# Natural-order loads of k and v, 64-row transposes and a direct wq product in a retention and token-mixing kernel

## The chip, the cores and the metric

The kernel runs on one core of one Trainium2 chip. The metric is device time in microseconds (us), the median of several runs of one launch. Profiled times come from one execution taken by the hardware profiler; its span begins and ends a little inside the time that is measured for the run.

## The reference

A recurrent retention layer (4 batches, 8 heads, 768 tokens, head size 64) is followed by a token-mixing layer on the 512 joined features. Inputs and output are 32-bit floats.

```
for t in range(S):                      # S = 768, per batch and head
    state = gamma[h] * state + outer(k[t], v[t])
    y[t]  = scale * q[t] @ state
x     = y, heads joined                 # (4, 768, 512)
wq, wk = x @ w_q, x @ w_k               # 512 -> 64
W_tok = scale * wq @ wk.T               # per batch, 768 x 768
out   = relu(W_tok @ x) @ w_out         # 512 -> 512
```

## The kernel before

The recurrence is computed in chunks of 128 tokens. Two chunks make a pair (256 tokens); there are 3 pairs in a batch and 12 in all, numbered 0 to 11. The decay factors are folded into v before the products and into y after them, so that within a chunk a masked matrix of scores does the work and between chunks a running state of 64x64 per head. The mixing layer never forms W_tok: z = wk.T @ x is summed over a batch's three pairs, and each pair's output follows from wq and z.

Every unit of work is a short named step of one pair. The list ORDER, written out in the file, is the order of the steps in the program: `name.pair.part:engine@bank`, with engines A (ScalarE, ACT in the profile), V (VectorE, DVE) and P (GpSimd, POOL); steps without a letter are matmuls (TensorE, PE). Each engine runs its own instructions strictly in this order, and waits where data or a buffer are not there. The steps of one pair, in the order in which data flow:

- `ck`, `cv`, `cq` cast k, v and q to 16 bits; `cv` also multiplies by the decay table `fv` (line 316, the other casts go through the helper of lines 137 and 138).
- `trk`, `trq` (lines 344, 359) transpose k and q on TensorE, 8 transposes of 128x128 each into one PSUM bank, and `ekT`, `eqT` copy them to SBUF.
- `sc` (line 379) makes the scores, `eat` (line 391) masks them with `cmask`; `st` (line 433) adds to the state, `es` copies it; `ia` (453) and `in` (419) make y from the scores and from the state; `ex` (467) scales y into `x`.
- `xt` (483) and `exT` transpose x. `wqk` (497) makes wq and wk in 8 matmuls; `ewq` and `ew` copy them out, `ewq` twice side by side; `tw` (523) transposes wq in two transposes and `ewt` copies the result.
- `zm` (545) and `ez` make z once per batch; `mx` (565), `r` (580, 582), `pj` (587) and `eo` make the output rows of a pair. `fill` (292) is matmuls on zeros, which keep TensorE active. `W` and `WO` cast weights.

Loads and stores go out on SyncE's queue (SP), in the order of the list LOADS: `k4` is a load of 512 KB, `w` and `o` are the weights, `s3` is a store of one pair's output. A load is written into one of 18 staging buffers, and is placed in the program behind the cast that frees the buffer. Each load reads runs of 512 bytes: two neighbouring tokens of one head lie side by side in one partition,

```
            in_=src[b, xs.start * HP : xs.stop * HP, cp * 2 * C : (cp + 1) * 2 * C, :].rearrange(
                "h (g j) d -> g h (j d)", j=2
```

so partition g holds tokens 2g and 2g+1 of the pair, and a chunk of 128 tokens lies in 64 partitions. The casts of k and v therefore take a chunk in two pieces of 64 partitions (even and odd tokens), and place these into the lower and the upper 64 partitions of the result. For every pair that is 4 instructions for k and 4 for v. Scores and masks use the same order of tokens (even ones first).

Of the kernel before, what the change touches and what calls it, by code (L numbers as in the profile page):

```python
# [16 lines left out]
ck.0.1:V cq.0.0:A ck.0.0:P fill.20@6 trk.0@6 cq.0.1:V trq.0@0 cv.0.0:V ekT.0:A eqT.0:A st.0.0  # L17
ck.1.1:V ck.1.0:A cv.0.1:P sc.0.0@0 eat.0.0:V es.0.0:A sc.0.1@2 eat.0.1:V fill.1@6 trk.1@6
cq.1:A fill.3@0 trq.1@0 st.0.1 cv.1.0:P ia.0.1@2 ekT.1:A ck.2.0:A in.0.1@2 eqT.1:V ia.0.0@2
sc.1.0@0 es.0.1:A sc.1.1@4 cq.2:A ck.2.1:P st.1.0 ex.0:V trk.2@6 cv.1.1:P trq.2@2 eat.1.1:V  # L20
es.1.0:A eat.1.0:V eqT.2:A ekT.2:V ck.3.1:A ck.3.0:A xt.0@4 st.1.1 sc.2.0@2 cv.2.0:P cq.3:A
sc.2.1@0 exT.0:V es.1.1:V cv.2.1:P ia.1.0@4 cv.3.0:P in.1.0@4 eat.2.0:V in.1.1@4 ia.1.1@4
cv.3.1:P ck.4.1:P ex.1:V st.2.0 in.2.0@2 fill.1@6 trk.3@6 es.2.0:A cv.4.0:P cv.4.1:P fill.1@4
trq.3@4 ekT.3:A eat.2.1:V W:A ia.2.0@2 eqT.3:V ia.2.1@2 in.2.1@2 xt.1@6 sc.3.0@4 ex.2:V st.3.0
wqk.0@0 xt.2@1 exT.1:A wqk.1@6 es.3.0:A sc.3.1@2 eat.3.0:V ewq.0:A in.3.1@4 exT.2:V st.3.1
wqk.2@1 ew.0:A cq.4:A ia.3.0@4 eat.3.1:V ewq.1:A ewq.2:V ew.2:V ia.3.1@4 tw.1@2 ex.3:V cv.5.0:P
ew.1:A ck.4.0:A trq.4@6 trk.4@3 tw.0@1 ewt.1:V tw.2@0 es.3.1:A ck.5.1:A ekT.4:V eqT.4:V ck.5.0:A
ewt.2:A xt.3@4 st.4.0 cq.5:A fill.2@2 sc.4.0@2 trk.5@6 ewt.0:A exT.3:V ekT.5:V zm.0@4 trq.5@5
ez.0:A cv.5.1:P WO:P sc.4.1@0 es.4.0:A eat.4.0:V st.4.1 cq.6:P mx.0@2 eat.4.1:V eqT.5:A cv.6.0:P
es.4.1:A sc.5.1@4 sc.5.0@0 r.0:A wqk.3@6 st.5.0 eat.5.1:V in.4.0@2 mx.2@4 eat.5.0:V ewq.3:A  # L30
ia.4.1@2 in.4.1@2 es.5.0:V ck.6.1:A ck.6.0:A r.2:A cv.6.1:P ia.4.0@2 ew.3:V ia.5.1@0 in.5.0@0
ex.4:V in.5.1@0 ia.5.0@0 ex.5:V pj.0.0@6 trk.6@2 xt.4@3 trq.6@4 ekT.6:V pj.0.1@5 eo.0.0:A xt.5@6
eqT.6:V mx.1@0 exT.4:A exT.5:V ck.7.0:A sc.6.0@2 eat.6.0:V ck.7.1:P r.1:A st.6.0 cv.7.0:P tw.3@4
pj.2.0@6 cq.7:A wqk.4@0 es.6.0:V ew.4:V eo.2.0:A sc.6.1@2 wqk.5@1 trq.7@6 eat.6.1:V ewt.3:A
trk.7@4 ew.5:V ewq.4:A st.6.1 ewq.5:A ekT.7:V cv.7.1:P eqT.7:A pj.1.0@1 tw.4@6 es.6.1:V eo.0.1:V
ia.6.1@2 ck.8.1:A eo.1.0:A ia.6.0@2 in.6.1@2 cv.8.1:P sc.7.0@4 ewt.4:V cq.8:A st.7.0 zm.1@6
sc.7.1@0 ex.6:V trq.8@2 es.7.0:A eat.7.0:V cv.8.0:P ez.1:A xt.6@6 ck.8.0:A pj.1.1@3 exT.6:V
eat.7.1:V trk.8@4 pj.2.1@6 mx.4@0 eqT.8:A eo.1.1:A mx.3@2 st.7.1 r.4:V ekT.8:A sc.8.0@4 eo.2.1:A
ck.9.1:P wqk.6@6 es.7.1:A cq.9:P r.3:A st.8.0 ck.10.0:P ewq.6:A ia.7.1@0 ew.6:A ia.7.0@0
sc.8.1@2 in.7.0@0 es.8.0:A in.7.1@0 eat.8.0:V cq.10:P eat.8.1:V in.8.0@4 ck.9.0:A in.8.1@4  # L40
pj.4.0@6 eo.4.0:A ck.10.1:A ex.7:V cv.9.0:P ia.8.0@4 ia.8.1@4 pj.3.0@2 tw.5@6 cv.9.1:P trk.9@3
ex.8:V ewt.5:A trq.9@0 trq.10@6 eqT.9:V eqT.10:V ekT.9:A xt.8@4 sc.9.0@0 eat.9.0:V st.9.0
trk.10@3 eo.3.0:A ekT.10:V pj.4.1@6 exT.8:A ck.11.0:P sc.9.1@0 ck.11.1:A mx.5@4 es.9.0:V
eat.9.1:V xt.7@3 wqk.8@2 eo.4.1:A trk.11@6 ia.9.1@0 r.5:A exT.7:A cq.11:P ia.9.0@0 in.9.1@0
ewq.8:V cv.10.0:P ew.8:A sc.10.0@4 cv.10.1:P st.9.1 tw.6@3 ekT.11:V cv.11.0:P wqk.7@6 trq.11@2
ex.9:V ewt.6:A tw.8@3 eat.10.0:V ew.7:A es.9.1:A eqT.11:A ewq.7:A ewt.8:V pj.3.1@0 eo.3.1:V
xt.9@1 sc.11.0@2 sc.10.1@4 exT.9:A pj.5.1@6 pj.5.0@1 tw.7@0 st.10.0 eat.11.0:V eat.10.1:V
eo.5.0:V eo.5.1:A ewt.7:V zm.2@6 es.10.0:A ez.2:A st.10.1 es.10.1:V in.10.1@4 sc.11.1@2
cv.11.1:P in.10.0@4 mx.6@0 ia.10.1@4 eat.11.1:V r.6:A wqk.9@6 ia.10.0@4 st.11.0 mx.7@0 ex.10:V
r.7:A pj.6.0@2 eo.6.0:A es.11.0:V ewq.9:V ia.11.1@4 ew.9:A ia.11.0@4 in.11.0@4 in.11.1@4 mx.8@0  # L50
xt.10@6 pj.6.1@2 ex.11:V exT.10:A xt.11@3 r.8:A wqk.10@6 eo.6.1:V exT.11:V pj.7.1@4 ew.10:V
ewq.10:V eo.7.1:A wqk.11@3 ew.11:A tw.9@6 pj.7.0@2 ewq.11:A tw.10@3 ewt.10:V zm.3@4 ewt.9:A
pj.8.0@6 ez.3:V tw.11@3 eo.7.0:A eo.8.0:A mx.10@4 mx.9@0 ewt.11:V mx.11@2 pj.8.1@6 r.10:A
pj.10.1@4 r.11:V pj.10.0@5 eo.10.1:V pj.11.1@2 pj.11.0@4 eo.8.1:A eo.10.0:A r.9:V pj.9.0@6
eo.9.0:A pj.9.1@5 eo.11.0:V eo.9.1:A eo.11.1:V
# [5 lines left out]
q0 v0 k1 q1 v1 k2 q2 v2 k3 q3 v3 w k4 q4 v4 k5 q5 v5 o k6 q6 v6 k7 q7 v7 k8 q8 v8 k9 q9 v9 k10  # L61
q10 s0 v10 k11 s1 q11 s2 v11 s4 s3 s5 s6 s7 s8 s10 s11/0 s11/1 s9
# [3 lines left out]
OBUFS = 10  # L66


@with_exitstack
def kernel(  # L70
# [9 lines left out]
):  # L80

# [9 lines left out]
    C = 128  # L91
# [27 lines left out]
    wqn_pool = pool("wqn", 3)  # L119
# [8 lines left out]
    def bank16(b):  # L128
        return banks[:, b, :].bitcast(BF16)
# [19 lines left out]
    def load(name, p, half=None, eng=None):  # L149
        src = {"k": k, "q": q, "v": v}[name]  # L150
        b, cp = divmod(p, NP)
        st = pairs[p]
        if name + "_st" not in st:
            st[name + "_st"] = stage_pool.tile([128, 2, HP, 2, D], FP32, name=name + "_st", tag="st")
        xs = slice(0, 2) if half is None else slice(half, half + 1)
        dma = (eng or nc.sync).dma_start(
            out=st[name + "_st"][:, xs].rearrange("g x hp j d -> g (x hp) (j d)"),
            in_=src[b, xs.start * HP : xs.stop * HP, cp * 2 * C : (cp + 1) * 2 * C, :].rearrange(
                "h (g j) d -> g h (j d)", j=2
            ),  # L160
        )
    def load_token(token):
        if token == "w":
            nc.sync.dma_start(out=wq_stage, in_=moe_w_q.rearrange("(a p) h -> p a h", p=128))
            nc.sync.dma_start(out=wk_stage, in_=moe_w_k.rearrange("(a p) h -> p a h", p=128))
        elif token == "o":
            for a in range(NDM):
                nc.sync.dma_start(
                    out=wout_stage[:, a], in_=moe_w_out[128 * a : 128 * a + 128, :], max_dma_last_dim=512
                )  # L170
        else:
            load(token[0], int(token[1:]))
# [10 lines left out]
    def more_loads():  # L183
        while queue:
# [6 lines left out]
            if token not in "wo":  # L191
                n = len(staged)
                if n >= STAGES and staged[n - STAGES] not in cast:
                    return
                staged.append(token)
# [53 lines left out]

    identity = const_pool.tile([128, 128], BF16, name="identity")  # L250
# [24 lines left out]
    wqk_sb = const_pool.tile([128, NDM, 2 * DH], BF16, name="wqk_w")  # L275
    wout_sb = const_pool.tile([128, NDM, DM], BF16, name="wout_sb")

    def W(e):
        copy(e, wqk_sb[:, :, 0:DH], wq_stage)
        if e == "A":  # L280
            nc.scalar.mul(out=wqk_sb[:, :, DH:], in_=wk_stage, mul=float(wk_scale))
        else:
            ENGINES[e].tensor_scalar_mul(
                out=wqk_sb[:, :, DH:], in0=wk_stage, scalar1=float(wk_scale)
# [14 lines left out]
    def ck(e, b, p, c):  # L299
# [3 lines left out]
        for j in range(2):  # L303
            copy(
                e,
                st["ks"][rows(j), c].rearrange("p hp x d -> p x hp d"),
                st["k_st"][rows(c), :, :, j],
# [3 lines left out]
    def cv(e, b, p, c):  # L311
        st = pairs[p]
        if "vs" not in st:
            st["vs"] = cast_pool.tile([128, 2, HP, 2, D], BF16, name="vs")
        for j in range(2):
            ENGINES[e].tensor_tensor(  # L316
                out=st["vs"][rows(j), c].rearrange("p hp x d -> p x hp d"),
                in0=st["v_st"][rows(c), :, :, j],
                in1=fv[rows(c), p % NP, :, j]
                .rearrange("p (x hp) -> p x hp", x=2)  # L320
                .to_broadcast([G, 2, HP, D]),
                op=ALU.mult,
            )
        release("v" + str(p), 2)
# [13 lines left out]

    def trk(e, b, p):
        st = pairs[p]  # L340
        ps = bank16(b).rearrange("p (hp c t) -> p hp c t", hp=HP, c=2)
        for c in range(2):
            for hp in range(HP):
                nc.tensor.transpose(  # L344
                    ps[:, hp, c], st["ks"][:, c, hp].rearrange("p x d -> p (x d)"), identity
                )
        st["ktr_ps"] = bank16(b)

    def ekT(e, b, p):
        st = pairs[p]  # L350
        st["kT"] = qkt_pool.tile([128, HP, 2, C], BF16, name="kT")
        copy(e, st["kT"].rearrange("p hp c t -> p (hp c t)"), st["ktr_ps"])

    def trq(e, b, p):
        st = pairs[p]
        ps = bank16(b).rearrange("p (hp c j g) -> p hp c j g", hp=HP, c=2, j=2)
        for hp in range(HP):
            for j in range(2):
                nc.tensor.transpose(  # L359
                    ps[:, hp, :, j, :],  # L360
                    st["qs"][:, hp, j].rearrange("p x d -> p (x d)"),
                    identity,
                )
        st["qtr_ps"] = bank16(b)

    def eqT(e, b, p):
        st = pairs[p]
        st["qT"] = qkt_pool.tile([128, HP, 2, C], BF16, name="qT")
        copy(e, st["qT"].rearrange("p hp c t -> p (hp c t)"), st["qtr_ps"])
# [18 lines left out]
    def eat(e, b, p, half):  # L388
# [5 lines left out]
            in1=cmask.rearrange("p o j t -> p o (j t)").to_broadcast([128, 8, C]),  # L394
# [271 lines left out]
```

## Time and profile before

| | before |
|---|---|
| median of 3 runs | 102.04 us (101.32 to 102.66) |
| the profiled execution, its time | 101.49 us |
| its span | 99.8 us |
| mean granted TensorE clock | 0.955 |
| busy: PE, DVE, ACT, POOL | 86.5, 75.3, 72.5, 66.8 us |
| packets of the load and store queue | 52592, 26.22 MB |
| read from and written to HBM | 20.19 MB and 6.29 MB |

The busy times are those of instructions on an engine, the share is of the span. Matmuls overlap each other, so their mean durations are latencies; how fast they follow each other is read from the chain of waits, where each piece runs from its release to the next one's. DMA rates are given in GB/s over a stretch, and the DMA share is the time of packets over sixteen engines, which goes above 1 where a packet starts before the one ahead has ended.

### The profile page before, as it was taken

Reading aid. Unit: us, or ns where it says so; the run is one execution under the profiler, and the core shown is the slowest. Engines: PE = TensorE matmul, PEld = TensorE weight load, DVE = VectorE, ACT = ScalarE, POOL = GpSimd, SP = SyncE. Lnnn points to the kernel's source line nnn. Section 1 sums busy time; section 2 is a strip of 40 time slices with the busy share of each in tenths; the row PEclk is TensorE's granted clock in tenths of the full one; section 3 lists DMA queues with packets and bytes.
Section 4 is the critical chain, followed back from the end, with each engine's and each line's share of the span. In section 5 each row is a group of like instructions: output and inputs, shape, how many; then the busy total and the mean of one; then the engine's idle time right before and its main releaser. Section 6 shows DMA issues by size and latency. Waiting matters only on the chain.

```text
span 99.8 us, 3208 instructions
## 1 busy us (share of the span) xinstructions
PE 86.5 (87%) x1319; PEld 60.0 (60%) x1332; DVE 75.3 (75%) x114; ACT 72.5 (73%) x123; POOL 66.8 (67%) x82
## 2 busy tenths in 40 slices
PE   4994669968999899989987999999899999999920
PEld 1344537857798666666865667768666776644400
DVE  3066972999999899967989678999969988227800
ACT  4126977199799996799899998999784567754130
POOL 6566589998969689769999999995699930000000
PEclk9999955699999999999999999999999999999995
DMA  1999999999999999999999999899967600762995
GB/s 22 283 348 347 347 347 349 285 253 276 323 298 295 327 290 322 270 312 336 338 343 346 323 300 305 255 317 341 290 204 217 204 13 7 210 210 69 317 290 167
DMA packets 53134, 26.68 MB, mean 267 GB/s; under 512 B 1920, under 2 KB 53120, under 8 KB 53120
## 3 DMA queue, kind: packets, MB, share of 16 engines
q1 hardware_dynamic: 52592, 26.22, 89.5%
q10 hardware_dynamic: 528, 0.26, 0.9%
q8 instruction: 10, 0.16, 0.6%
q14 instruction: 4, 0.03, 0.1%
HBM read 20.19 MB, written 6.29 MB: 265 GB/s over the span
## 4 chain that ended last, share of the span: by engine, by line
PE 41%; DVE 23%; DMA 14%; ACT 10%; issue 5%; SPq 1%; POOL 1%; ACTq 0%; DVEq 0%; POOLq 0%
PE banks L587 16%; DVE at_sb L391 11%; DMA q_st<-in_q_dram 7%; DMA v_st<-in_v_dram 6%; PE banks L453 4%; ACT ks L137 4%; DVE x_nat L467 4%; PE banks L483 3%; PE banks L379 3%; ACT o_st L137 3%; PE banks L497 2%; DVE vs L316 2%; PE banks L359 2%; PE banks L419 2%; PE banks L433 2%
## 5 line engine op out<-in xcount | busy, mean ns | idle before, releaser
L316 POOL TENSOR_TENSOR vs<-v_st,fv 64x512 bf16<-64x512 f32 x46 | 48.9, 1062 | 8.3 <-DMA v_st<-in_v_dram 3.7
L391 DVE TENSOR_TENSOR at_sb<-banks,cmask 128x1024 bf16<-128x1024 f32 x24 | 28.8, 1218 | 0.6 <-ACT s_sb L137 0.4
L587 PE MATMUL banks<-wout_sb,relu 128*128 128x512 bf16 x86 | 22.5, 379 | 0.8 <-ACT wqn L137 0.2
L137 ACT CAST ks<-k_st 64x512 bf16<-64x512 f32 x30 | 18.6, 619 | 1.8 <-DMA k_st<-in_k_dram 1.5
L467 DVE TENSOR_TENSOR x_nat<-banks,fy 128x1024 bf16<-128x1024 f32 x12 | 14.5, 1220 | 2.1 <-PE banks L453 1.1
L137 ACT COPY o_st<-banks 128x512 f32<-128x512 f32 x17 | 10.0, 589 | 6.6 <-PE banks L587 6.4
L587 PEld LDWEIGHTS <-relu 128*128 128x128 bf16 x96 | 8.5, 98 | 8.5 <-issue 0.8
L137 ACT CAST qs<-q_st 128x1024 bf16<-128x1024 f32 (+1 forms) x8 | 8.0, 996 | 3.7 <-DMA q_st<-in_q_dram 3.7
L292 PE MATMUL banks<-warm 128*128 128x512 bf16 x25 | 8.8, 507 | 2.1 <-DVE warm L211 1.3
L379 PE MATMUL banks<-qT,kT 64*128 64x128 bf16 x192 | 9.2, 225 | 1.4 <-DVE kT L138 0.9
L580 ACT ACTIVATE relu<-banks 128x1024 bf16<-128x1024 f32 x9 | 9.3, 1035 | 1.2 <-PE banks L565 1.2
L138 POOL CAST ks<-k_st 64x512 bf16<-64x512 f32 x14 | 8.9, 633 | 1.6 <-DMA k_st<-in_k_dram 1.0
L453 PE MATMUL banks<-vs,at_sb 128*128 128x64 bf16 x192 | 9.0, 197 | 0.3 <-DVE at_sb L391 0.2
L344 PE MATMUL banks<-identity,ks 128*128 128x128 bf16 x96 | 7.8, 224 | 1.0 <-ACT ks L137 0.6
L359 PE MATMUL banks<-identity,qs 128*128 128x128 bf16 x96 | 7.8, 227 | 1.0 <-ACT qs L137 0.5
L453 PEld LDWEIGHTS <-at_sb 128*128 128x128 bf16 x192 | 7.3, 100 | 1.8 <-DVE at_sb L391 0.5
L379 PEld LDWEIGHTS <-kT 64*128 64x128 bf16 x192 | 6.0, 98 | 3.7 <-issue 1.3
L433 PE MATMUL banks<-vs,ks 128*64 128x64 bf16 x160 | 6.5, 205 | 1.8 <-DVE vs L316 1.8
L359 PEld LDWEIGHTS <-qs 128*128 128x128 bf16 x96 | 6.3, 102 | 2.7 <-ACT qs L137 1.1
L483 PE MATMUL banks<-identity,x_nat 128*128 128x128 bf16 x96 | 7.4, 219 | 0.1
L344 PEld LDWEIGHTS <-ks 128*128 128x128 bf16 x96 | 6.1, 100 | 2.3 <-ACT ks L137 1.3
L497 PE MATMUL banks<-wqk_w,xT 128*128 128x128 bf16 x96 | 7.4, 219 | 0.1
(60 smaller groups left out, 123.2 us busy)
## 6 DMA issues: line engine op xcount, KB each, us to landing
q_st<-in_q_dram SPq DMA_DIRECT2D x12, 512.0 KB, 6.3
v_st<-in_v_dram SPq DMA_DIRECT2D x12, 512.0 KB, 6.5
k_st<-in_k_dram SPq DMA_DIRECT2D x11, 512.0 KB, 6.2
out_dram<-o_st SPq DMA_DIRECT2D x11, 512.0 KB, 3.3
wout_stage<-in_moe_w_out_dram SPq DMA_DIRECT2D x4, 256.0 KB, 5.3
out_dram<-o_st SPq DMA_DIRECT2D x2, 256.0 KB, 2.3
k_st<-in_k_dram ACTq DMA_DIRECT2D x1, 256.0 KB, 4.3
k_st<-in_k_dram SPq DMA_DIRECT2D x1, 256.0 KB, 4.0
```

The costliest lines, as they stand in the source:

```text
L137: return nc.scalar.copy(out=out, in_=in_)
L316: ENGINES[e].tensor_tensor(out=st["vs"][rows(j), c].rearrange("p hp x d -> p x hp d"), in0=st["v_st"][rows(c), :, :, j], in1=fv[rows(c), p ...
L344: nc.tensor.transpose(ps[:, hp, c], st["ks"][:, c, hp].rearrange("p x d -> p (x d)"), identity)
L359: nc.tensor.transpose(ps[:, hp, :, j, :], st["qs"][:, hp, j].rearrange("p x d -> p (x d)"), identity,)
L379: nc.tensor.matmul(out=ps[:, x, hi, c, :], lhsT=st["kT"][rows(x), hp, c, :], rhs=st["qT"][rows(x), hp, c, :], start=(hi == 0 and c == 0), ...
L391: ENGINES[e].tensor_tensor(out=st["at", half].rearrange("p x hi c t -> p (x hi c) t"), in0=st["at_ps", half].rearrange("p (n t) -> p n t", ...
L453: nc.tensor.matmul(out=y[:, x, c, hp, :], lhsT=st["at", half][:, x, hi, c, :], rhs=st["vs"][:, c, hp, x, :], start=first(p, x), stop=False ...
L467: nc.vector.tensor_tensor(out=st["x"].rearrange("p x c i n -> p (x c i n)").rearrange("p (m d) -> p m d", d=D), in0=st["y_ps"].rearrange(" ...
L483: nc.tensor.transpose(ps[:, a, c, :], st["x"][:, a // 2, c, a % 2, :], identity)
L497: nc.tensor.matmul(out=ps[:, c, :], lhsT=st["xT"][:, a, c, :], rhs=wqk_sb[:, a, :], start=(c == 0 and a == 0), stop=(a == NDM - 1), skip_g ...
L580: nc.scalar.activation(out=dst, in_=st["mx_ps"], func=ACT.Relu)
L587: nc.tensor.matmul(out=bank32(b), lhsT=st["relu"][:, a, j, :], rhs=wout_sb[:, a, :], start=(a == 0), stop=(a == NDM - 1),)
```

## The change

- `load`: k and v of pairs 3 to 11 (those not in `TWO`) are loaded chunk by chunk in natural order, token t of a chunk in partition t, as two transfers of 256 KB each with runs of 256 bytes. q, and all of pairs 0 to 2, stay as they were.
- `ck`, `cv`: for these pairs a chunk of k is cast in one instruction over 128 partitions, and both chunks of v (for pair 11 each by itself) in one. New tables `fvn` and `cmaskn` hold the decay and the mask for natural order; the step `N` makes them on POOL and ACT.
- `trk`, `trq`, `xt`: each 128x128 transpose is split into two transposes of 64 rows, whose results go to two PSUM banks. k and q of one pair share two banks. The copies `ekT`, `eqT` and `exT` read from both banks.
- `wqk`: wq is made transposed and twice over by 4 matmuls with the weights as the stationary operand, wk as before by 8 matmuls of 64 columns. One copy `ew` takes all 384 columns out; `ewq`, `tw` and `ewt` are gone, and `mx` reads wq with a permuted pattern.
- ORDER and LOADS are new. In LOADS all stores stand behind the last load, and `w` stands ahead of pair 3.

```diff
 LOADS = """
-q0 v0 k1 q1 v1 k2 q2 v2 k3 q3 v3 w k4 q4 v4 k5 q5 v5 o k6 q6 v6 k7 q7 v7 k8 q8 v8 k9 q9 v9 k10
-q10 s0 v10 k11 s1 q11 s2 v11 s4 s3 s5 s6 s7 s8 s10 s11/0 s11/1 s9
+q0 v0 k1 q1 v1 k2 q2 v2 w k3.0 k3.1 q3 v3.0 v3.1 k4.0 k4.1 q4 v4.0 v4.1 k5.0 k5.1 q5 v5.0 v5.1 o
...
+k10.0 k10.1 q10 v10.0 v10.1 k11.0 k11.1 q11 v11.0 v11.1 s0 s1 s2 s3 s5 s4 s7 s6 s8 s9 s10 s11/1
+s11/0
...
+TWO = (0, 1, 2)
...
+        if natural:
+            t0 = cp * 2 * C + part * C
+            dst = st[name + "_st"][:, part]
+            source = src[b, :, t0 : t0 + C, :].rearrange("h p d -> p h d")
...
+    def natural_tables():
+        nc.gpsimd.iota(
+            tvn,
...
+        for c in range(2):
+            nc.gpsimd.tensor_tensor(
+                out=tvn[:, :, c], in0=tvn[:, :, c], in1=ln_v[:, :, :, 0], op=ALU.mult
+            )
...
+        nc.gpsimd.affine_select(
+            out=cmaskn,
...
+        nc.scalar.activation(out=fvn, in_=tvn, func=ACT.Exp)
...
     def ck(e, b, p, c):
...
+            copy(
+                e,
+                st["ks"][:, c].rearrange("p hp x d -> p x hp d"),
+                st["k_st"][:, c].rearrange("p (x hp) d -> p x hp d", x=2),
+            )
...
+    def cv(e, b, p, c=None):
...
+            cs = slice(0, 2) if c is None else slice(c, c + 1)
+            n = (cs.stop - cs.start) * H
             ENGINES[e].tensor_tensor(
+                out=st["vs"][:, cs].rearrange("p c x hp d -> p (c x hp) d"),
+                in0=st["v_st"][:, cs].rearrange("p c h d -> p (c h) d"),
+                in1=fvn[:, cp, cs].rearrange("p c h -> p (c h)").to_broadcast([128, n, D]),
...
     def trk(e, b, p):
         st = pairs[p]
-        ps = bank16(b).rearrange("p (hp c t) -> p hp c t", hp=HP, c=2)
+        ps = tr_of(p, b)[:, :, 0:512].rearrange("p r (hp c g) -> p r hp c g", hp=HP, c=2)
         for c in range(2):
             for hp in range(HP):
-                nc.tensor.transpose(
-                    ps[:, hp, c], st["ks"][:, c, hp].rearrange("p x d -> p (x d)"), identity
-                )
+                for r in range(2):
+                    nc.tensor.transpose(
+                        ps[:, r, hp, c],
+                        st["ks"][rows(r), c, hp].rearrange("p x d -> p (x d)"),
+                        diagonal(r),
+                    )
...
     def wqk(e, b, p):
         st = pairs[p]
-        ps = bank32(b)[:, 0:256].rearrange("p (c n) -> p c n", c=2)
+        ps = bank32(b)[:, 0:384]
+        for a in range(NDM):
+            nc.tensor.matmul(
+                out=ps[:, 128:384],
+                lhsT=wqk_sb[:, a, 0:128],
+                rhs=st["xT"][:, a].rearrange("p c t -> p (c t)"),
...
         for c in range(2):
             for a in range(NDM):
                 nc.tensor.matmul(
-                    out=ps[:, c, :],
+                    out=ps[:, c * DH : (c + 1) * DH],
                     lhsT=st["xT"][:, a, c, :],
-                    rhs=wqk_sb[:, a, :],
-                    start=(c == 0 and a == 0),
+                    rhs=wqk_sb[:, a, 128:192],
+                    start=False,
...
     def ew(e, b, p):
         st = pairs[p]
-        st["wk"] = moe_pool.tile([128, 2, DH], BF16, name="wk_n")
-        copy(e, st["wk"], st["wqk_ps"][:, :, DH:])
+        st["w"] = moe_pool.tile([128, 384], BF16, name="w_x")
+        copy(e, st["w"], st["wqk_ps"])
```

## The prediction

> **What bounds the kernel now.** I read the page first: busy times, then the 40 slices.
>
> ```profile
> PE 86.5 (87%) x1319; PEld 60.0 (60%) x1332; DVE 75.3 (75%) x114; ACT 72.5 (73%) x123; POOL 66.8 (67%) x82
> PE   4994669968999899989987999999899999999920
> PEclk9999955699999999999999999999999999999995
> DMA  1999999999999999999999999899967600762995
> ```
>
> No engine is idle for long and the DMA row is full for 28 slices (70 us). So I asked for busy time by stretches (columns: PE, PEld, DVE, ACT, POOL, then clock, DMA share, GB/s).
>
> ```profile
> 9.00:19.00 10.00, 7.34 (x103) 5.36 (x104) 7.60 (x8) 7.36 (x12) 8.17 (x9) 0.67 1.15 345
> 22.00:22.80 0.80, 0.80 (x32) 0.65 (x26) 0.80 (x3) 0.79 (x2) 0.80 (x1) 1.00 1.05 243
> 30.00:60.00 30.00, 27.59 (x474) 20.14 (x477) 25.74 (x35) 27.60 (x49) 26.30 (x27) 1.00 1.08 317
> 80.00:90.00 10.00, 9.84 (x119) 6.21 (x121) 5.26 (x11) 6.98 (x12) 0.65 (x1) 1.00 0.36 108
> ```
>
> Three stages show. To about 20 us the loads set the pace (345 GB/s, the best rate there is). From 20 to 70 us all of PE, ACT, POOL and DVE are 86 to 92% busy, and loads run at 317. From 72 to 95.4 us PE alone is the bound. The chain of waits agrees: its last 25 us are matmuls (columns: start, us, what).
>
> ```profile
> 1.84 6.36 DMA v_st<-in_v_dram
> 22.22 0.36 PE banks L453 x8
> 22.59 0.34 PE banks L419 x16
> 22.93 0.34 PE banks L453 x8
> 23.27 0.26 PE banks L433 x8
> 43.60 0.45 PE banks L483 x8
> 80.82 0.47 PE banks L453 x16
> 89.21 6.17 PE banks L587 x28
> 95.40 0.59 ACT o_st L137
> ```
>
> The chain also gives PE's true pace, which mean durations (latencies of some 200 ns) hide: 8 transposes 0.45 us, 8 `sc` matmuls 0.33, 4 `pj` matmuls 0.86, and so on. After PE's end at 95.4 come 4.4 us: eviction, last store, end of the program.
>
> **PE's part of the change.** Per pair by these paces: trk, trq, xt 0.45 each; sc 0.66; st 0.48; ia 0.50; in 0.34; wqk 0.45; tw 0.11; zm 0.24; mx 0.33; pj 1.72: 6.18 us. A 64-row transpose becomes 16 instructions with a 64x128 weight and 64 moving columns. That is the shape of the `in` matmuls (L419), 16 of which took 0.34: I take 0.33, so three steps save 0.36 us. The new wqk has 4 matmuls of 256 columns (half of `pj`'s 512, so 0.43) and 8 of 64 columns (as `st`, 0.24): 0.68 in all, against 0.45+0.11. Net 0.24 us saved per pair, 2.9 in all, to 5.94 a pair. Fills rise from 28 to 32 (0.9 us at 0.216).
>
> Against it stands the change between 64-row and 128-row instructions. L453 takes 0.47 for 16 in one run, but 0.34 to 0.36 for 8 between L419 steps: 0.11 more for two changes, 0.06 each. Counting the written order, such changes go from 85 to 103: 1.1 us lost. If one cost nothing the sum gains 1.1, and if it cost the full 0.11 it loses another 0.9. So PE alone gains 2.9-1.1-0.9 = 0.9 us.
>
> The Trainium skill's TensorEngine Tiling (Array Packing), Key Properties, says that a change of tiling mode (not just of tile) drains the array. The 0.06 us above is what this trace shows of that; were a drain as long as a whole `in` matmul record (193 ns), 18 more changes would cost 3.5 us in place of 1.1, as an estimate.
>
> **The vector engines.** A 64x512 piece costs as much as a 128x512 one (the row for ks on ACT 619 ns, a 128x512 qs on ACT 618), so whole casts halve the work. For nine pairs: k 9x2x0.62 = 11 us, v 9x(4x1.06-2.1) = 19 us (one 128x1024 multiply at twice the 64x512 row).
>
> ```profile
> L316 POOL TENSOR_TENSOR vs<-v_st,fv 64x512 bf16<-64x512 f32 x46 | 48.9, 1062 | 8.3 <-DMA v_st<-in_v_dram 3.7 <-PE banks L344 1.7 <-PE banks L453 0.4
> L137 ACT CAST ks<-k_st 64x512 bf16<-64x512 f32 x30 | 18.6, 619 | 1.8 <-DMA k_st<-in_k_dram 1.5
> ```
>
> wqn, wk_n and wqT (392+298+380 ns on ACT) become one 128x384 eviction, about 0.49 between the 128x256 and 128x512 rows: 0.55 a pair, 7 us. Summed over the new order: POOL 64 to 40 us, ACT 78 to 66, DVE 79 to 76. ACT and POOL no longer hold PE from 20 to 70 us; POOL's backlog (8.8 us without a pause from 71.83, casting v for pairs 10 and 11) goes. DVE stays near full, so I count no more gain than PE's shorter waits. The evictions of transposes now read two banks in runs of 64; same element count, so I cost them at nothing, and at 10% more they would add 3 us shared by ACT and DVE, covered by ACT's relief.
>
> **Early stage.** ACT's new Exp for `fvn` waits for POOL's iota and two multiplies, which stand behind cq.1, which waits for q1 (v0 lands at 8.20, two loads later is 11.2): 11.2+1.04+0.43+0.42 = 13.1. Behind it on ACT stand ck.1.1, es.0.0, ck.1.0 (3.1 us) and PE's trk.1, so trk.1 starts near 16.4 instead of 11.5. Work from trk.1 to PE's end is 68.5 us by the paces; with 1.045 (below) 71.6, ending at 88.0. That is 4 us earlier than the path found below, which covers it. Past that cover each us counts in full. The half clock at 12 to 19 us (PEclk 5) may stay away with the added fills; no gain is counted, since this stage waits for loads.
>
> **The loads, which decide.** k and v of pairs 3 to 11 now move in runs of 256 bytes, 2048 packets per 512 KB in place of 1024. The only 256-byte loads before are wq and wk. Their packets on one DMA engine start 14.1 ns apart in unbroken runs in the trace's packet records, where 512-byte packets start 23.5 ns apart. Low end: 2048x14.1/16 = 1.81 us per 512 KB (290 GB/s). High end: the mean over those loads, 243 GB/s in 22.00:22.80, 2.16 us. I take 1.81: other packets and refilling queues lie in that mean, and such losses I add apart, as 345/317 = 1.09 on everything after 18 us. A 512-byte load takes 1.52.
>
> Landings: v0 at 8.20, six loads on v2 at 17.3, w 1.1 later (18.4). A pair is then (1.52+2x1.81)x1.09 = 5.6 us; wout 3.3. So v5 35.2, v6 44.1, v8 55.3, v11 72.1. SP now issues 36 DMAs of 1024 packets for these 18 loads; an issue that nothing blocks took 0.49 to 0.57 us (q0 and v0 in SP's timeline), so two take 1.1 and lie beside the 1.81 of transfer; only at faster transfers than that would SP set the pace. The stage pool is never late (a load needs the cast from six pairs before), and all stores now come behind v11: 18 us of transfers, of which half are ready by then and half wait for `eo` anyway.
>
> The skill's DMA: Bandwidth & Descriptors, Specifications, asks for at least 512 bytes for line rate and says that smaller ones are done as read-modify-write. This trace has 290 to 243 GB/s at 256 bytes, so it agrees in sign; if a small packet cost as much as a 512-byte one, a load would take 3.04 us and the whole time would be near 122 us, an estimate.
>
> **The sum.** Adding the paces down the written order from a step to the end gives the PE work left there. Before, trk.9 starts at 63.46 with 30.9 us left, and PE ends 31.9 later: 1.03. With 18 more changes in 72 us: 1.045. After the last piece of v8 POOL needs 2.1+0.2, then st.8.0 begins with 33.3 us of paced work left: 55.3+2.3+33.3x1.045 = 92.4. For pair 11 POOL takes the piece that lands last first (two of 1.06): 72.1+2.3+16.1x1.03 = 91.0. Pairs 6, 7 and 9 end between 91 and 92.4 as well. PE's end 92.4 plus 4.4 gives a span of 96.8. The profiled execution took 101.49 for a span of 99.8, so 98.5; the median shown (102.04) lies 0.55 above that execution: **99.0 us**, 3% faster. With every pair near the bound, 2 us of jitter is likely on either side: 97.0 to 101.0 for this case.
>
> **Rivals.**
> Loads at the wq/wk mean (2.16): v11 lands at 79.0, PE ends at 97.9, span 102.3, **104.5 us, slower**. It decides from 2.03 us per load (258 GB/s), where pair 11 alone gives PE's end of before. For it: 0.8 us of records average 243. Against: the spacing in the runs.
> PE stays the bound and its waits stay (DVE as full as before): only the 0.9 us come, 98.9 span, **101.1 us, no change**. For it: PE 92% busy, more mode changes. Against: 12 us off ACT, 24 off POOL.
> Better than forecast: without the loss factor v8 lands at 52.3, so PE could end at 89.4: span 93.8, **96.0 us**; against it, every stretch past 20 us in which loads ran below 345.
>
> **How the numbers follow.** Forecast 0.48, slower loads 0.22, PE-bound 0.22, better 0.08. A measurement of this kernel tells about 2% from no change: faster means below 100.0, slower above 104.1. The forecast's case gives faster in 0.42, same in 0.06; the better one 0.08; PE-bound same 0.19, slower 0.01, faster 0.02; slow loads same 0.05, slower 0.17. Together 0.52, 0.30, 0.18. Range 96.0 to 104.5, from the better case to the price of slow loads.
>
> **What would show it.** Right: loads at 280 GB/s or more between 20 and 60 us, v11 landed by 73, the POOL row near 40 us, transposes at 0.33 per 16, PE ending near 92. Wrong: a DMA row full past 76 us with PE waiting for ks, qs or vs; or PE above 92% busy from 20 us with 0.45 per transpose step, which makes PE the bound; or trk.1 later than 20 us.

## The result and the profile after

| | before | changed |
|---|---|---|
| median (range), of these runs | 101.68 us (99.94 to 102.66, 4 runs) | 108.91 us (108.36 to 112.16, 4 runs) |
| ratio, 95% interval | 1 | 1.081 [1.065, 1.097] |

The change makes the kernel 8% slower; 99.0 us was forecast, so the sign was wrong and the time is outside the range. The profiled execution of the changed kernel took 112.16 us (span 110.5), which is the longest of its runs; its clock was granted at 0.938, and rates are read from it rather than the total (`e5_wide_transposes` below, with the same loads and 108.65 us, gave 245 GB/s from 20 to 60 us, this execution 239).

From the page of the changed kernel: busy times, then slices.

```profile
PE 86.2 (78%) x1634; PEld 57.3 (52%) x1648; DVE 72.2 (65%) x102; ACT 63.0 (57%) x101; POOL 42.1 (38%) x54
PE   5993755889679879978689685992799979999930
DMA  1999999699979998998969999989999992074995
GB/s 22 325 347 347 347 342 262 196 284 269 215 176 271 245 282 202 278 209 206 298 158 270 259 245 211 224 223 206 259 250 346 341 346 73 0 241 145 285 320 154
```

ACT and POOL came down as the sum of rows said (63 and 42 us), and yet, apart from DVE between 30 and 40 us, no engine is full in the middle: PE is at 6 to 9 tenths in most slices. The DMA row is nearly full to slice 33, or 91 us (loads to 83 us, then stores), where before it was nearly full to slice 29, or 72 us. From slice 7 to slice 30 its transfers run at 158 to 298 GB/s only. The stretches (columns: PE, PEld, DVE, ACT, POOL, clock, DMA share, GB/s) show the same:

```profile
30.00:40.00 10.00, 7.57 (x220) 6.38 (x222) 9.55 (x11) 5.22 (x10) 3.45 (x4) 1.00 0.92 231
50.00:60.00 10.00, 8.34 (x185) 6.09 (x186) 7.85 (x10) 6.27 (x12) 4.68 (x4) 1.00 0.92 228
70.00:80.00 10.00, 7.16 (x134) 5.30 (x132) 6.14 (x8) 5.96 (x9) 4.05 (x3) 0.86 0.92 228
```

SyncE's own queue in the timeline (start, length) shows when the two loads of k of pairs 8 to 11, and at last of v of pair 11, were issued.

```profile
52.11 2.48 SPq L170 DMA_DIRECT2D k_st<-in_k_dram  x2
59.13 2.25 SPq L170 DMA_DIRECT2D k_st<-in_k_dram  x2
66.30 2.19 SPq L170 DMA_DIRECT2D k_st<-in_k_dram  x2
73.62 2.28 SPq L170 DMA_DIRECT2D k_st<-in_k_dram  x2
77.03 2.97 SPq L170 DMA_DIRECT2D v_st<-in_v_dram  x2
```

Here a pair takes (73.62-52.11)/3 = 7.2 us. The forecast had 5.6, its slow rival 6.4. POOL's cast of v of pair 11, which waits for the last piece, starts at 83.44 us, so v11 is there at 83.4 and not at 72.1. The waits of POOL (us in total, times, the longest) and the chain of waits follow from it:

```profile
POOL vs L382 <- DMA v_st<-in_v_dram: 16.3, 5, 5.6
POOL qs L140 <- DMA q_st<-in_q_dram: 13.2, 6, 3.8
```

```profile
61.47 6.15 DMA q_st<-in_q_dram
67.64 0.02 POOLq L140
67.74 0.84 POOL qs L140
68.58 6.60 DMA q_st<-in_q_dram
```

Before, the chain's middle held PE, DVE and ACT. Now, from 48.6 to 75.2 us, it goes from one load of q to the next, with little more than a cast between; from 12 to 45 us it is still PE, DVE and ACT, and it starts with the Exp for `fvn`. The full DMA row past 76 us is the first of the signs that the forecast named for being wrong.

### The profile page after: what moved, and what is told of

The parts are those of the page before. It is cut to its first block, busy times and chain, and to the rows that moved or that the text cites. A ratio compares the mean times of both kernels' runs of the same rounds, so it can differ in the third digit from the quotient of the medians.

```text
span 110.5 us, 3791 instructions
## 1 busy us (share of the span) xinstructions
PE 86.2 (78%) x1634; PEld 57.3 (52%) x1648; DVE 72.2 (65%) x102; ACT 63.0 (57%) x101; POOL 42.1 (38%) x54
## 2 busy tenths in 40 slices
DMA packets 71857, 26.73 MB, mean 242 GB/s; under 512 B 39072, under 2 KB 71840, under 8 KB 71840
## 4 chain that ended last, share of the span: by engine, by line
PE 32%; DMA 26%; DVE 13%; ACT 9%; issue 8%; POOL 4%; SPq 3%; DVEq 0%; POOLq 0%
DMA q_st<-in_q_dram 26%; PE banks L665 12%; DVE at_sb L475 6%; ACT kT L139 4%; SPq L170 3%; POOL qs L140 3%; PE banks L539 3%; PE banks L440 3%; PE banks L463 3%; DVE qT L140 2%; ACT ks L139 2%; DVE x_nat L553 2%; PE banks L590 2%; PE banks L419 2%; PE banks L621 2%
## 5 line engine op out<-in xcount | busy, mean ns | idle before, releaser
L382 POOL TENSOR_TENSOR vs<-v_st,fvn 128x1024 bf16<-128x1024 f32 (+1 forms) x10 | 17.3, 1731 | 24.9 <-DMA v_st<-in_v_dram 16.3
L475 DVE TENSOR_TENSOR at_sb<-banks,cmaskn 128x1024 bf16<-128x1024 f32 x18 | 21.4, 1219 | 3.4 <-PE banks L463 3.4
L139 ACT CAST ks<-k_st 64x512 bf16<-64x512 f32 (+1 forms) x20 | 12.1, 618 | 5.2 <-DMA k_st<-in_k_dram 5.0
L337 PE MATMUL banks<-warm 128*128 128x512 bf16 x30 | 10.3, 476 | 4.0 <-DVE warm L222 1.3
L139 ACT COPY kT<-banks 128x1024 bf16<-128x1024 bf16 x9 | 9.1, 1016 | 7.1 <-PE banks L440 3.2
L658 ACT ACTIVATE relu<-banks 128x1024 bf16<-128x1024 f32 x11 | 11.3, 1033 | 3.0 <-PE banks L665 1.7
L140 POOL CAST qs<-q_st 128x1024 bf16<-128x1024 f32 (+1 forms) x7 | 6.9, 979 | 14.0 <-DMA q_st<-in_q_dram 13.2
L139 ACT CAST s_sb<-banks 128x256 bf16<-128x256 f32 x17 | 6.4, 377 | 8.4 <-PE banks L519 8.4
L140 DVE COPY o_st<-banks 128x512 f32<-128x512 f32 x10 | 6.9, 688 | 5.3 <-PE banks L665 5.2
L140 DVE COPY qT<-banks 128x1024 bf16<-128x1024 bf16 x8 | 5.5, 690 | 5.8 <-ACT kT L139 2.9
L475 DVE TENSOR_TENSOR at_sb<-banks,cmask 128x1024 bf16<-128x1024 f32 x6 | 7.1, 1218 | 2.9 <-ACT fvn L289 2.2
L371 POOL TENSOR_TENSOR vs<-v_st,fv 64x512 bf16<-64x512 f32 x8 | 8.3, 1043 | 0.5
```

What stands on the lines that cost most here:

```text
L139: return nc.scalar.copy(out=out, in_=in_)
L140: return ENGINES[e].tensor_copy(out=out, in_=in_)
L337: nc.tensor.matmul(out=bank32(b), lhsT=warm[:, 0:128], rhs=warm, start=True, stop=True)
L371: ENGINES[e].tensor_tensor(out=st["vs"][rows(j), c], in0=st["v_st"][rows(c), :, :, j], in1=fv[rows(c), cp, :, j] .rearrange("p (x hp) -> p ...
L382: ENGINES[e].tensor_tensor(out=st["vs"][:, cs].rearrange("p c x hp d -> p (c x hp) d"), in0=st["v_st"][:, cs].rearrange("p c h d -> p (c h ...
L475: ENGINES[e].tensor_tensor(out=st["at", half].rearrange("p x hi c t -> p (x hi c) t"), in0=st["at_ps", half].rearrange("p (n t) -> p n t", ...
```

## The experiments

### Loads in long runs, everything else as changed

`e1_all_512` sets `TWO` to all pairs: one load of 512 KB in runs of 512 bytes, and the casts in halves again.

> The changed kernel with k and v of all pairs loaded in runs of 512 bytes again, as q is (and cast in halves of 64 partitions); transposes, wq product and order stay those of the change. Theory L (the 256-byte loads are the whole loss): loads go back to about 310 GB/s between 20 and 60 us, the last lands near 70 us, and the time falls to between 98 and 102 us. Theory C (the new order or the 64-row transposes lose the time, and the loads only look late): it stays above 105 us although the loads are fast.

Measured: 108.40 us (107.31 to 108.89). Loads were quick (303 GB/s from 20 to 60 us), but POOL now had little slack in an order paced for the short casts. Its stretch from 30 to 80 us (POOL is the fifth engine):

```profile
30.00:80.00 50.00, 42.03 (x936) 30.23 (x936) 42.35 (x48) 36.09 (x56) 45.75 (x47) 0.97 0.92 269
```

Only 2% of this run's chain of waits lies on POOL itself, so that POOL replaced the loads as the bound is not shown. The run changes loads and casts together and settles nothing about the loads alone. `e7_long_runs_same_casts` does, as it changes only how the bytes are fetched:

```diff
-            t0 = cp * 2 * C + part * C
-            dst = st[name + "_st"][:, part]
-            source = src[b, :, t0 : t0 + C, :].rearrange("h p d -> p h d")
+            if part == 1:
+                return
+            dst = st[name + "_st"].rearrange("p c (h j) d -> p (c h) (j d)", j=2)
+            source = src[b, :, cp * 2 * C : (cp + 1) * 2 * C, :].rearrange("h (g j) d -> g h (j d)", j=2)
```

> The changed kernel with everything as it is (whole casts, order, transposes, wq product), except that each load of k and v of pairs 3 to 11 is one transfer of 512 KB in runs of 512 bytes into the same buffer; tokens and heads then lie elsewhere in it, which changes the output and none of the work on the engines. Theory L (the 256-byte loads are the whole loss): the last load lands by 70 us and the time falls to between 96 and 100 us, my forecast without its load term. Theory C (the new order loses time by itself, as all loads at 512 bytes still took 108.4 us): the loads are early and the time stays above 104 us.

Measured: 105.32 us, ratio 1.037 [1.028, 1.046]. In this order the natural loads cost 3.6 us of some 7.2 by the medians, 4.4 of 8.1% by the ratios; the rest has another cause. Loads ran at 298 GB/s from 20 to 60 us, better than the forecast's pace (three loads of 512 KB in 5.6 us, 281 GB/s), and PE still ended at 98.9 us, not 92.4. In this run's chain the only load is the first one. Behind it come the new Exp, pair 1's transposes of k (L420), and then PE, DVE and ACT to the end:

```profile
12.81 0.24 ACT fvn L290
...
16.06 0.40 PE banks L420 x15
...
96.76 2.12 PE banks L666 x9
```

### The loads by themselves

`e3_loads_alone` keeps the loads and casts and drops all of TensorE's work and what depends on it; the stored output is zeros. `e4_loads_alone_512` is the same with `TWO` for all pairs.

> Only the loads and the casts of the changed kernel, then stores of zeros; all matmuls, masks, copies out of PSUM and the output's arithmetic are left out, so TensorE runs no program and fetches no instructions. Theory Q (what queues for the DMA engines is a fixed number of packets, and 256-byte packets run it empty): the rate between 20 and 60 us stays near 240 GB/s with the same gaps, and the last load lands near 80 us. Theory F (TensorE's instruction fetches, 0.9 us each on one DMA engine, open the gaps): no gaps, 290 GB/s where all packets have 256 bytes, the last load lands by 70 us.

> As the run before it, loads and casts alone, but with runs of 512 bytes for all pairs. Theory Q: 345 GB/s or a little less, the last load lands near 61 us. Theory F: 345 GB/s throughout, the last load lands near 60 us, 9 us earlier than with all the work beside it.

Measured: 99.78 and 85.27 us (one execution each, as for the next two runs). The stretch from 20 to 60 us, natural first and long runs second (DVE, ACT, POOL, clock, DMA share, GB/s):

```profile
20.00:60.00 40.00, 2.33 (x3) 4.76 (x9) 21.61 (x17) 1.00 1.06 261
```

```profile
20.00:60.00 40.00, 4.74 (x6) 13.03 (x22) 38.09 (x39) 1.00 1.15 346
```

With nothing else on the core the natural loads reach 261 GB/s, 6.3 us per pair of loads of k to the next. The packet records show where it goes. A microsecond filled with 256-byte packets holds up to 1125 of them (288 GB/s: the spacing of 14.1 ns was right), but after one or two such microseconds the counts fall. In the changed kernel the packets per microsecond from 53 us on are 1100, 1082, 911, 831 and 174. So the rate in unbroken runs is not the rate that lasts. TensorE fetches no instructions in the first of these runs and the thin stretches are there all the same, so Theory F does not explain them.

Two runs asked whether one issuing queue is the limit. Both are `e3_loads_alone` with one line more in `load`, for natural loads of v: `eng = nc.scalar` in the first, `eng = nc.gpsimd` in the second.

> Loads and casts alone as in the first such run, with the 18 natural loads of v issued on ScalarE's queue instead of SyncE's; nothing else. Theory Q (the packets that one issuing queue holds run out): with two queues the all-256-byte stretches hold 285 GB/s without gaps and the last load lands 4 to 8 us earlier than 77 us. Theory E (the sixteen DMA engines themselves pause on 256-byte packets): the same 230 to 280 GB/s, the last load at 75 us or later.

> The same with the loads of v issued on GpSimd's queue. Theory Q: no gaps and an earlier last load, as with ScalarE's queue, unless GpSimd spends so long on each issue that its casts of v come late. Theory E: the rate stays at 230 to 280 GB/s.

Measured: 92.71 and 93.56 us. The first, in the same stretch:

```profile
20.00:60.00 40.00, 8.57 (x7) 13.25 (x23) 30.04 (x23) 1.00 1.23 308
```

The same packets of 256 bytes (39072 of them, 39073 in `e3_loads_alone`) go at 308 GB/s from two queues and at 261 from one, with 62 and 60% of the bytes of the stretch in such packets; the counts stay near 1125 per microsecond where nearly all are short, and the last short packet starts at 65.8 us in place of 76.6. The memory and the DMA engines can take the faster rate; one queue does not keep it up. That is shown for the loads alone. The second run is not so clean: GpSimd's queue turned the loads of v into fewer, larger packets (54563 packets in all in place of 71844), which was not foreseen.

### Transposes

`e5_wide_transposes` puts 128x128 transposes back into the changed kernel, k in one bank and q in the other:

```diff
-        ps = tr_of(p, b)[:, :, 0:512].rearrange("p r (hp c g) -> p r hp c g", hp=HP, c=2)
+        ps = tr_of(p, b)[:, 0].rearrange("p (hp c t) -> p hp c t", hp=HP, c=2)
...
-                for r in range(2):
-                    nc.tensor.transpose(
+                nc.tensor.transpose(ps[:, hp, c], st["ks"][:, c, hp].rearrange("p x d -> p (x d)"), identity)
...
```

> The changed kernel with its 256-byte loads, but with transposes of 128x128 as before (k in one bank of the two, q in the other). 576 TensorE instructions fewer of 3298, so two instruction fetches of 16 KB fewer of 13. Theory Q: the loads set the end, the time stays within 1 us. Theory F: each fetch costs the loads 1 to 1.5 us, so the time falls by 2 to 3 us. Theory C (64-row transposes lose): it falls by more.

Measured: 108.19 us (107.46 to 108.67), 0.7 us below the changed kernel, whose runs lie between 108.36 and 112.16: with slow loads the transposes matter little. `e12_long_runs_wide_transposes` has the same edit on `e7_long_runs_same_casts`.

> The kernel of e7_long_runs_same_casts (changed kernel, k and v of pairs 3 to 11 fetched in runs of 512 bytes into the same buffers, so values sit in the wrong places and the output is another) with 128x128 transposes, k in one PSUM bank and q in the other. With long runs alone it was 105.3 us, and the waits of TensorE for the copies kT and qT were the longest left. Theory B (k and q sharing two banks makes each copy and the next transposes wait for one another): the row of TensorE waiting for kT in the second transposes falls from 1.7 us to nearly 0, the copies become one-bank copies, and the time falls to 100 to 102 us, although the transposes take 0.12 us more per step (about 3.5 us of TensorE in all). Theory C (the new order's distances between steps, whatever the banks): it stays at 104 to 107 us, the waits move to other rows.

Measured: 103.32 us, ratio 1.020 [1.006, 1.035], 2.0 us better than `e7_long_runs_same_casts`, though PE's row rose from 83.6 to 88.0 us. The profiled executions differ in granted clock (0.960 and 1.000), but two others with 0.978 and 0.983 took 105.20 and 103.28 us. What had been lost is in the chain of `e7_long_runs_same_casts`: the transposes of q (L441) and the copy of q wait for the copy of k, in the banks that k and q share.

```profile
60.25 1.02 ACT kT L139
61.27 0.02 issue
61.29 0.70 DVE qT L140
```

Its waits of PE, and then the corresponding ones of `e12_long_runs_wide_transposes` (L452 is the scores, L464 above):

```profile
PE banks L464 <- DVE qT L140: 1.9, 4, 0.9
PE banks L441 <- ACT kT L139: 1.7, 2, 1.1
PE banks L464 <- ACT kT L139: 1.7, 2, 1.3
```

```profile
PE banks L452 <- DVE qT L140: 0.9, 2, 0.6
```

The waits of the q transposes and of the scores for kT are gone. The edit takes back two things at once (the 64-row form, with its changes between 64 and 128 rows, and the shared banks). Since the 64-row form is the shorter one in PE's row, and these waits go, the gain is put down to the banks; no run changes the banks alone.

### The old order

`e9_natural_old_order` is the kernel before with natural loads and whole casts for pairs 3 to 11 and nothing else changed. `e15_old_order_long_runs` is the same with its loads in runs of 512 bytes into the same buffers.

> The kernel before with natural-order loads and whole casts of k and v for pairs 3 to 11 alone (one instruction per chunk), with the old order, the old transposes and the old wq. Theory L: the loads fall behind as in the changed kernel (near 240 GB/s, last load past 82 us, since stores lie between them here) and the time is 106 to 112 us. Theory C: the loads are late but the old order hides it, the time stays within 2% of before.

> The kernel before in its old order, with 128x128 transposes and the old wq product, with whole casts of k and v of pairs 3 to 11, and with these loads made in runs of 512 bytes (512 KB each) into the same buffers, so that values sit in the wrong places and the output is another. It is e9_natural_old_order (114.8 us) with the loads' cost taken out. Theory L (the loads are all that makes e9 slow, and whole casts gain what the forecast gave them in part): 97 to 101 us, GpSimd's row near 40 us. Rival O (the old order has no use for shorter casts): 101 to 103 us, PE's row and waits as before. Rival W (a whole cast waits for the last of the data where a half cast could begin, or POOL and VectorE disturb each other more): 104 us or more.

Measured: 114.79 us, ratio 1.116 [1.098, 1.134], and 101.91 us, ratio 1.013 [1.004, 1.022]. By the ratios natural loads cost the old order 10.3%, the new one 4.4%: the new order loses less by them. And with long runs, whole casts gave nothing, although POOL went from 66.8 to 45.4 us. Loads still lie on the chain of `e15_old_order_long_runs` up to 43.6 us (296 GB/s from 20 to 60 us, 310 before), so this run alone does not show what bounds it. `e21_old_order_all_savings` adds the new wq product and leaves out `ewq`, `tw` and `ewt`.

> The kernel of e15_old_order_long_runs (old order, 128x128 transposes, whole casts, long runs into the same buffers, so that values sit in the wrong places and the output is another) with the new wq product and without ewq, tw and ewt. It has every copy and cast that the change saves, fast loads and no shared banks. Theory P (TensorE paces, and copies of the other engines are off its path): 100.5 to 102 us, TensorE's row no lower than 86.5 us and its waits under 8 us, though GpSimd, ScalarE and VectorE together have 30 us less than before. Rival (the savings were real and only the loads and the new order hid them): 96 to 99 us.

Measured: 101.65 us, ratio 1.004 [0.998, 1.011]. It has every saving of copies, quick loads and no shared banks. From 20 to 60 us:

```profile
20.00:60.00 40.00, 37.92 (x736) 29.05 (x735) 36.35 (x44) 29.47 (x48) 21.15 (x22) 1.00 1.07 315
```

ACT and POOL have 21 us less to do here than before (29.5 and 21.2 against 36.8 and 34.7), and PE is 95% busy against 91%; 73% of the chain lies on PE, 41% before, and no load. TensorE was the bound, and the relief was off its path. Part of the shorter waits probably went into the wider product: PE's row is 87.7 us, 87.0 in `e15_old_order_long_runs`. That product alone on the kernel before, twice, the second time in more rounds:

> The kernel before with one part of the change alone: wq made transposed and twice over by its product, one copy of 384 columns, and the steps ewq, tw and ewt taken out of the order; all else, loads and order too, as before. Theory A (the evictions and TensorE pieces saved are worth what the forecast gave them, 7 us of copies and 0.1 us of TensorE a pair less the longer wait for one copy): 98.5 to 101 us, ScalarE and VectorE rows 3 to 4 us lower each. Rival (off the path): 101.5 to 102.5 us. Rival (the wider product costs TensorE, which paces): 103 us and TensorE's row higher by 1 to 2 us.

> The kernel of e14_before_new_wq_product unchanged (100.9 us, ratio 0.9887 with an interval that reached 1.0033), complete and correct, timed in more rounds. Theory A (a gain of 1 us, from copies taken off the end of the kernel where ScalarE and VectorE set the pace): ratio 0.985 to 0.995. Rival (chance): 0.995 to 1.005.

Measured: 100.91 us, ratio 0.989 [0.974, 1.003], and 101.86 us, ratio 1.013 [1.007, 1.019]. The two do not agree about the sign of 1%: the interval of the first includes 1, that of the second, from 12 executions, lies above it. No gain is claimed; if anything the product costs a little here.

### Two queues in the complete kernel

The loads of v are issued by another engine some pairs ahead of their use, as a step `lv` in the order. On ScalarE, for the changed kernel and for `e9_natural_old_order`:

```diff
+    def lv(e, b, p):
+        for c in range(2):
+            load("v", p, c, ENGINES[e])
...
+        if natural and name == "v" and eng is None:
+            return
...
-es.0.0:A sc.0.1@2
+es.0.0:A lv.3:A sc.0.1@2
```

> The changed kernel, complete, with the natural loads of v of pairs 3 to 11 issued by ScalarE instead of SyncE, three to four pairs ahead of their use. Theory Q (one issuing queue cannot keep enough 256-byte packets in flight): 284 to 305 GB/s in the middle instead of 228 to 259, last landing of v near 72 us instead of 84, and the time falls towards that of e7_long_runs_same_casts, 104 to 106 us (ScalarE gives 18 issues of 0.38 us, 7 us of its time). Rival (the memory side or instruction fetches set the rate whatever the queue): the rates stay under 260 GB/s and the time at 108 to 109 us, or above it by ScalarE's 7 us.

> The kernel of e9_natural_old_order (kernel before with natural loads and whole casts of k and v of pairs 3 to 11, old order, 114.8 us) with the natural loads of v issued by ScalarE instead of SyncE. Theory Q: loads at 284 to 305 GB/s and the time falls by 8 to 12 us to 103 to 107 us; below 102 only if the whole casts gain on the old order. Rival (rate set by the memory side): 113 to 116 us.

Measured: 132.31 and 126.17 us, both far worse and for a reason that no theory named. The first one's longest wait on ACT:

```profile
ACT ks L138 <- DMA wout_stage<-in_moe_w_out_dram: 17.0, 1, 17.0
```

ScalarE's stream stood for 17 us (20.9 in the second run) at its first load of v until a load issued earlier in the program had landed, and all its casts stood behind it. The trace gives that load as the releaser; the likely reading is that the program ties a new DMA to the end of one listed before it, which was not tried. In the first run loads went at 290 to 310 GB/s from 20 to 50 us, in the second at 263, 303 and 258 in these three stretches of 10 us, with most of the other work standing still. So the runs don't speak against the queue theory; they don't time it either. On GpSimd, ahead of the cast of v three pairs earlier, for the changed kernel, for `e9_natural_old_order`, and for the changed kernel with 128x128 transposes:

> The changed kernel, complete, with the natural loads of v of pairs 3 to 11 issued by GpSimd instead of SyncE, each ahead of the cast of v three pairs earlier. Theory Q (one queue cannot keep enough packets in flight): loads of k, q and v at 284 to 310 GB/s between 20 and 60 us, the last v landed by about 70 us, and the time 104.5 to 106.5 us, that is the 3.5 us that long runs gave, with GpSimd giving 18 issues of 0.9 us. Rival (memory side or fetches limit the rate): under 260 GB/s and 108 to 110 us. Rival (GpSimd's issues wait for something as ScalarE's did): 110 us or more, with GpSimd's queue waiting on a DMA for many us.

> The kernel before in its old order with natural loads and whole casts of k and v of pairs 3 to 11 (e9_natural_old_order, 114.8 us, is the same with one queue), the natural loads of v issued by GpSimd, ahead of the cast of v three pairs earlier. A complete kernel. Theory Q with L: the time comes down to 1 to 4 us above e15_old_order_long_runs, that is 99 to 105 us; if both hold fully, at or below the kernel before. Rival (rate set by the memory side): 113 to 116 us.

> The changed kernel, complete, with the natural loads of v issued by GpSimd (as e17_after_v_on_POOL_queue) and with 128x128 transposes, k in one bank and q in another (as e5_wide_transposes and e12_long_runs_wide_transposes). If loads and banks are the two causes and add up: 102.5 to 105 us, near the 103.3 of e12, whose loads are a little faster. Rival (banks matter only while loads are as fast as in e12): within 0.5 us of e17.

Measured: 108.72 us (1.075 [1.062, 1.088]), 105.67 us (1.050 [1.039, 1.060]) and 107.46 us (1.073 [1.065, 1.081]). In the old order 6.6 of the 10.3% came back. In the new one nothing clear of the intervals did, with shared or with separate banks, although the last load of k was issued at 63 us in place of 74. Its GpSimd pays for it (group of its load issues, and its stretch from 30 to 40 us):

```profile
L171 POOL DMA_DIRECT2D v_st<-in_v_dram x18 | 16.5, 917 | 0.0
```

```profile
30.00:40.00 10.00, 7.70 (x209) 6.29 (x210) 9.05 (x11) 4.92 (x10) 9.97 (x10) 1.00 1.07 314
```

POOL is nearly without a pause from 20 to 50 us (9.6, 10.0 and 10.0 us of each 10), and 19% of the chain lies on it, 4% in the changed kernel. As these loads also travel in larger packets here, the runs don't separate the queue from the packet size. No version with natural loads and the right output beat the kernel before.

## Why the prediction was wrong

**The step that failed: the loads.** The term was (1.52+2x1.81)x1.09 = 5.6 us per pair. With the forecast's own 18.4 and 3.3 us, v11 at 83.4 means (83.4-18.4-3.3)/9 = 6.9 us per pair on average, and 7.2 was read for the last ones. The spacing of 14.1 ns was right, the choice between the two ends was not: the low end came from unbroken runs, and the mean of 243 GB/s over wq and wk was set aside as holding other packets and refilling queues. Such thin stretches are just what a long series of these loads has too. The rival said that loads decide from 2.03 us per natural load, or (1.52+2x2.03)x1.09 = 6.1 us a pair. It named the right cause, but its 2.16 us with the same losses (6.4 us a pair) was still too quick: 6.9 to 7.2 us a pair means (6.9/1.09-1.52)/2 = 2.4 to 2.5 us. From v11 on the sum held: 83.4 and 2.3+16.1x1.03 = 18.9 us of work behind it put PE's end at 102.3. In `e5_wide_transposes`, with v11 at 82.4, PE ended at 102.5; in this execution it ended at 106.0, with a granted clock of 0.80 from 80 to 90 us.

**SP beside the transfers.** The forecast let two issues take 1.1 us beside the transfer. They took 2.2 to 3 us. Already in the 512-byte loads at the start an issue lasts about as long as a transfer (1.45 us against 1.52) once the first few are under way, where the first three took 0.43 to 0.57. We read this as SP waiting for room in its queue: the same limit seen from SP's side, not one more cost.

The Trainium skill's DMA: Bandwidth & Descriptors, Issuing engines are not separate DMA queues, says that issuing from several engines saves only the time that the issuing takes. The loads alone gained more here: 308 against 261 GB/s for the same 256-byte packets, 92.7 against 99.8 us. With 512-byte packets one queue already gave 346, the best rate seen; no run here tried a second queue there.

**The second step that failed: less work on ACT and POOL as shorter waits of PE.** The forecast took PE at 1.045 times its paces once the others were relieved. `e21_old_order_all_savings` has that relief without the cost, and is no faster than before; the rival "PE stays the bound" named the mechanism. In the new order PE was 85% busy from 20 to 60 us even with fast loads (34.17 of 40 in `e7_long_runs_same_casts`). This is the larger part of the miss: with loads faster than forecast that run took 105.3 us, 6.3 above the forecast.

The delay at the start belongs here. The forecast gave the work from pair 1's transposes of k to PE's end 68.5x1.045 = 71.6 us, so that a late start at 16.4 was covered. By the records that work took 83.8 us before (11.5 to 95.4), 82.8 in `e7_long_runs_same_casts` (16.1 to 98.9) and 81.2 in `e12_long_runs_wide_transposes` (15.9 to 97.2). The factor 1.045 was built on the last 32 us, where PE alone is the bound, and was used for the whole kernel. So the start came some 4.5 us later and the work behind it got only 1.0 to 2.6 us shorter. With quick loads the delay is not covered: it stands on the chain. In the old-order runs the tables are made ahead of all steps, and these transposes start at 11.3 to 11.9 us.

**The banks.** The copies from two banks were costed at nothing, and by themselves that was right: kT on ACT took 1018 ns before and 1016 after, qT on DVE 687 and 690. What was missed is that k and q now share the pair of banks, so the copy of q and q's transposes queue behind the copy of k. With 4.4 us less on PE's row in `e7_long_runs_same_casts` than in `e12_long_runs_wide_transposes`, the kernel was still 2 us slower; that the banks alone do this is argued, as said above.

**What held.** In the chain after, from 25 us on, 16 transposes of 64 rows take 0.23 to 0.36 us where PE runs on (0.33 forecast), and 0.42 or more behind a wait:

```profile
15.98 0.61 PE banks L419 x14
...
28.76 0.36 PE banks L440 x16
...
32.59 0.25 PE banks L419 x16
...
34.30 0.34 PE banks L440 x16
...
38.34 0.42 PE banks L419 x16
```

POOL and ACT fell to 42 and 63 us (40 and 66 forecast; before, the page has 66.8 and 72.5, where the forecast's sums had 64 and 78). The first transposes of pair 1 began at 15.98 us (16.4 forecast), behind the Exp for `fvn` as described.

**What stays open.** Of the 8.1%, long runs give back 4.4 and the wide transposes in separate banks 1.7 by the ratios; 2.0% [0.6, 3.5] remain. By the traces the late start of pair 1's transposes is large enough for that, but no run moved the step `N`, so this is read and not tested. Why one queue runs short of 256-byte packets is not shown: it may be a bound on packets or on transfers in flight. In the complete kernel loads are slower than alone (239 against 261 GB/s from 20 to 60 us); instruction fetches begin at 55.2, 61.5 and 71.9 us and thin stretches lie behind the first and the last, but no run of the complete kernel took them away.

## What to carry to other kernels

Take the rate of small packets from a stretch as long as the series that is planned, gaps included, and price every other loss on top of it. Before counting relief of other engines as gain, ask how busy the pacing engine is in that stage: at 91% there were few waits to win. A delay that is held for covered must be checked against every path behind it, with waits in its price. When two products are put into one pair of PSUM banks, follow who waits for whose eviction; the copies' own times do not show it.

## What the runs showed of the hardware

- From one queue, packets of 256 bytes reach 284 to 288 GB/s for a microsecond or two, and a mix with 60% of its bytes in such packets keeps 261 over 40 us; from SyncE's and ScalarE's queues together a mix with 62% keeps 308. Loads in 512-byte packets alone run at 346 from one queue.
- The same loads issued by GpSimd left 20640 packets under 512 bytes in place of 39073, at 0.92 us of GpSimd's time for each 256 KB.
- A copy of 128x1024 16-bit values out of PSUM costs the same from one bank as from two (1018 and 1016 ns on ACT).
